# A spectral filter and a low-rank mixer on one core: the start's loads and first-stage work re-ordered

## The chip, the core and the metric

The kernel runs on one core of a Trainium2 chip. A core has a matrix engine (TensorE, PE in the profile), a vector engine (VectorE, DVE), a scalar engine (ScalarE, ACT), a general engine (GpSimd, POOL), a queue processor (SyncE, SP) and 16 DMA engines that all queues share. Each engine runs its own instructions strictly in order; semaphores tie them together. The metric is the device time of one execution in microseconds. Before the change it is 557.71 us, the median of 3 runs (556.44 to 557.84).

## The reference

Two stages on `x` of 8 batches, 3136 positions, 256 channels:

```python
X = np.fft.rfft(x, axis=1)
Y = X * (filt_r + 1j * filt_i)
y = np.fft.irfft(Y, n=3136, axis=1)            # spectral filter
xt = y.transpose(0, 2, 1)
h = xt @ U @ V                                  # low rank over positions, rank 32
u = y + h.transpose(0, 2, 1)
out = u + np.maximum(u @ w_ch1, 0) @ w_ch2      # 256 -> 1024 -> 256
```

Inputs and output are float32; the kernel computes in float16 with float32 sums.

## The kernel before, in words

The length 3136 is split as 64 x 49, and the transform is made in two stages of matmuls.

**First stage** (`f1_units`, L392): 64-point transforms over one factor. The batch's x is loaded in four chunks (`load_x`, L133, two DMAs each, cast to float16 by POOL's queue). 13 units, each one matmul (L401) and one copy out of PSUM (L405 on DVE or L407 on ACT), give the array `c1` in DRAM; when a chunk's units (3, 3, 3 and 4) are done, two DMAs write the chunk (L411), from SP for batch 1 and from POOL for the others.

**Pairs** (`stream`, L462): 16 steps a batch, each for two of 32 residues. `load_a` (L418) brings eight residues in a tile `a2`, on SP's queue. A step makes the 49-point transform (`forward`, L435), the product with the filters on DVE (`both_products`, L443, for batches 0 and 1; `product`, L454 to L459, for the rest) and, two steps later (`LAG`), the inverse 49-point transform `i1` (L471) and its copy (L475). After every fourth pair SP writes the result to `c2` (L477), and `load_e` (L423) reads it back as a quarter of `e2` with two DMAs on SP, when that write has landed.

**Mixer**: `h1_unit` (L497) multiplies all of a batch's e2 with the transformed U (`usb`): 25 matmuls (L502). `make_u` (L544) finishes the inverse transform with the constant `s2` and adds the low-rank part (matmuls L524 and L529, copies L554). `mm1` (L556) and `mm2` (L570) are the two layers of the channel network, in groups of 4 x 128 positions; 6 such groups make a batch, and `out` is written group by group.

**Order.** The schedule is written by hand. First comes batch 0's spectral part by itself: `first_f1`, then `first_mid` (L331), which runs batch 0's 16 pairs without DRAM between: at pair m, the product of m, `back` of m-1 (L345, L348), `ahead` of m+2 and `first_a` of m+3 (L326, L328). The filters come in four parts (`PARTS`); DVE makes their swapped halves before pairs 4, 8 and 12 (L186, L193). Units of batch 1's first stage are put between: `next(fill)`. After pair 15 seven groups of transposes (L382, copies L384) make batch 0's e2, with `prep_u` (L262, transform of U into `usb`) and more units between them. Then batch 0's h1 and first u.

From there the rest runs in slots: two slots go with every two `mm1` tiles, 8 slots a group, `SB` = 48 slots a batch. `put(slot, ...)` hangs a piece of work into a slot: the list `steps` has the slot of each pair; loads of a2 stand some slots ahead of the pair that needs them, `load_e` 3 (batch 1) or 4 slots behind a quarter's last inverse transform, h1 of batch b in slot 48 b - 4, first-stage units of batch b ahead of its pairs, V's arrangement (`vgen`) in slots 1, 3, ..., 11. PE executes the slots in order, so a piece that waits there holds everything behind it. In the text, a(b, g) is the load of a2 for batch b and quarter g, e(b, g) that of e2, "unit" is a unit of the first stage.

The loads of the start stand in one queue on POOL (L196 to L227): batch 0's x, the rest of the filters' rows, then the four parts of filters and tables (`t2`, `g12`), batch 1's x, U, V, w1, w2 and s2. `keep_on(n)` (L280) issues n matmuls of constants whose result is not used.

Of the kernel before, what the change touches and what calls it, by code (L numbers as in the profile page):

```python
# [9 lines left out]
F16 = mybir.dt.float16  # L10
# [7 lines left out]
RANK = 32  # L18
# [68 lines left out]
def kernel(  # L87
# [11 lines left out]
    nc = tc.nc  # L99
# [100 lines left out]
        load_x(0, c)  # L200
    sel = cst.tile([32, 128], F16)
    nc.sync.dma_start(sel, sel_d.ap())
    for k, part in enumerate(PARTS):
        if k == 3:
            for c in range(2):
                load_x(1, c)
        if k:
            load_table(0, *part)
        load_filters(*part)
        if k == 0:  # L210
            load_table(0, *part)
        load_table(1, *part)
    for c in range(2, len(CH)):
        load_x(1, c)
    uq = sb.tile([64, NR * RANK], F16, tag="esb", bufs=2, name="uq")
    nc.gpsimd.dma_start(uq, moe_U.rearrange("(q r) p -> q (r p)", q=NQ))
    vqs = []
    for k in range(2):
        v = sb.tile([32, SEQ // 2], F16, tag="xt", bufs=8, name="vq")
# [1 line left out]
        nc.gpsimd.dma_start(v, moe_V[:, k * (SEQ // 2):(k + 1) * (SEQ // 2)])  # L221
    w1 = cst.tile([128, 2 * 1024], F16)
    nc.gpsimd.dma_start(w1, moe_w_ch1.rearrange("(h dd) c -> dd h c", h=2))
    w2 = cst.tile([128, 8 * DM], F16)
    nc.gpsimd.dma_start(w2, moe_w_ch2.rearrange("(t cc) e -> cc t e", t=8))
    s2 = cst.tile([128, 128], F16)
    nc.gpsimd.dma_start(s2, s2_d.ap())  # L227
    vr = cst.tile([128, NH * 128], F16)
    usb = cst.tile([128, NH * RANK], F16)
    nc.vector.memset(usb[64:128, (NH - 1) * RANK:NH * RANK], 0.0)  # L230
# [31 lines left out]
    def prep_u():  # L262
        for n0, nn in ((0, 16), (16, 9)):
            pu = bank("o", "pu")
            for h in range(2):
                m = (min(nn, NH - h - n0)) * RANK
                a = (h * NH + n0) * RANK
                nc.tensor.matmul(pu[64 * h:64 * h + 64, 0:m], w64[0:64, 0:64], uq[:, a:a + m],
                                 start=True, stop=True)
            m = (min(nn, NH - 1 - n0)) * RANK  # L270
            nc.scalar.copy(usb[:, n0 * RANK:n0 * RANK + m], pu[:, 0:m])
            if m < nn * RANK:
                nc.vector.tensor_copy(usb[0:64, n0 * RANK + m:(n0 + nn) * RANK],
                                      pu[0:64, m:nn * RANK])


# [54 lines left out]
    def first_mid(fill):  # L331

        et = sb.tile([128, 2 * NH * 128], F16, tag="e2", bufs=2, name="et")
        etv = et.rearrange("p (e r h k) -> p h e r k", e=2, h=2, k=64)
        pend = None

        def back(m, uv):
            pi = bank("fx"[m % 2], "pi")
            for sl in range(2):
                for dh in range(2):  # L340
                    for fi in range(2):
                        g = (4 * m + 2 * sl + fi) * 98
                        o = fi * 512 + sl * DM + dh * 128
                        a = (dh * 2 + sl) * 98
                        nc.tensor.matmul(pi[:, a:a + 98], uv[:, o:o + 128], g12[:, g:g + 98],  # L345
                                         start=(fi == 0), stop=(fi == 1), skip_group_check=True)
            for h in range(2):
                nc.scalar.copy(  # L348
                    etv[:, h, :, 0:NH - h, 4 * m:4 * m + 4],
                    pi[:, 0:392].rearrange("p (e k r) -> p e r k", e=2, r=NR)  # L350
                    [:, :, h * NH:h * NH + NH - h])

        def ahead(m):
            return forward(m, st[0]["a"][m // 4], ("m",))

        pxs = [ahead(0), ahead(1)]
        keep_on(8)
        for m in range(NS // 2):
            for k, part in enumerate(PARTS):
                if k and 2 * m == part[0]:  # L360
                    swap_real(*part)
                    swap_imag(*part)
            uv = both_products(m, pxs.pop(0))
            if pend is not None:
                back(*pend)
            pend = (m, uv)
            if m + 2 < NS // 2:
                pxs.append(ahead(m + 2))
            if m + 3 < NS // 2:
                first_a(m + 3)  # L370
            if m >= 7:
                next(fill)
        back(*pend)
        e2 = new_e2(0)
        for k4, n0 in enumerate(range(0, NH, 4)):
            pt = ps.tile([128, 1024], F16, tag="m", bufs=BUFS["m"], name="pe")
            w = min(4, NH - n0)
            k = 64 if w == 1 else 128
            for rr in range(w):
                for dh in range(2):  # L380
                    o, a = rr * DM + dh * 128, (dh * NH + n0 + rr) * 128
                    nc.tensor.transpose(pt[0:k, o:o + 128], et[:, a:a + k], idn[:, :])  # L382
            dst = e2[0:k, n0 * DM:(n0 + w) * DM]
            (nc.scalar.copy if k4 in (1, 4, 6) else nc.vector.tensor_copy)(dst, pt[0:k, 0:w * DM])  # L384
            if k4 == 1:
                prep_u()
            if k4 in (1, 2, 3, 4):
                next(fill)
            if k4 == 5:
                next(vgen)  # L390

    def f1_units(b, both):  # L392
        ne = 0
        for c in range(len(CH)):
            xt = st[b]["x"].pop(c)
            asb = sb.tile([128, 7 * DM], F16, tag="asb", bufs=3, name="asb")
            for n0 in range(0, CH[c], 2):
                w = min(2, CH[c] - n0) * DM
                k = 64 if c0[c] + n0 == NH - 1 else 128
                pf = bank("o" if b == 1 else "m", "pf")  # L400
                nc.tensor.matmul(pf[0:k, 0:w], w64[0:k, 0:k], xt[0:k, n0 * DM:n0 * DM + w],  # L401
                                 start=True, stop=True)
                dst = asb[0:k, n0 * DM:n0 * DM + w]
                if both and ne % 2 and (b > 1 or ne >= 9):
                    nc.vector.tensor_copy(dst, pf[0:k, 0:w])  # L405
                else:
                    nc.scalar.copy(dst, pf[0:k, 0:w])  # L407
                ne += 1
                if n0 + 2 >= CH[c]:
                    for h, o, n in span(c0[c], c0[c + 1]):  # L410
                        (nc.sync if b == 1 else nc.gpsimd).dma_start(c1[b].ap()[:, o:o + n], asb[64 * h:64 * h + 64, 0:n])  # L411
                yield
# [218 lines left out]
    next(h1_unit(0))  # L631
    make_u(0)

    steps = [9 + 1.5 * k for k in range(NP)] + [33 + 2.87 * k for k in range(NP)]
    for b in range(3, nb):
        steps += [SB * (b - 2) + 31 + 3 * k for k in range(NP)]
    steps += [steps[-1] + 3 * (k + 1) for k in range(LAG)]
# [6 lines left out]
    for b in range(1, nb):  # L644
        for gi in range(NS // KG):
            t = steps[NP * (b - 1) + GP * gi]
            put(t - 9, one(load_a, b, gi))
        put(SB * b - 4, h1_unit(b))
        if b > 1:
            fill = f1_units(b, b == 2)  # L650
            for k in range(NF):
                put(4 + 1.1 * k if b == 2 else steps[NP * (b - 1)] - 49 + 3 * k, fill)
            for c in range(len(CH)):
                if b == 2 and c > 1:
                    put(3 * c - 2, one(load_x, b, c))
# [55 lines left out]
```

## Time and profile before

| | |
|---|---|
| median of 3 runs | 557.71 us (556.44 to 557.84) |
| profiled execution | 560.07 us, of which the profile's span is 558.3 us |
| PE busy | 529.5 us (95%) |
| DVE, ACT, POOL busy | 366.9, 363.1, 248.8 us (66%, 65%, 45%) |
| mean granted clock of PE | 0.988 |
| first mm1 matmul (L561) | 56.35 us |
| PE busy from 0 to 55 us | about 37 us |

The slices of the page are 14 us wide, 40 over the span. Lines of a timeline read: start, duration, engine, line, operation, tiles, shapes, and in brackets the engine's idle time before it with what ended the idle time. "SPq" is the issue of a DMA; the transfer itself ends later. Lines of a chain read: start, duration, what.

### The profile page before, as it was taken

Reading aid. Unit: us, or ns where it says so; the run is one execution under the profiler, and the core shown is the slowest. Engines: PE = TensorE matmul, PEld = TensorE weight load, DVE = VectorE, ACT = ScalarE, POOL = GpSimd, SP = SyncE. Lnnn points to the kernel's source line nnn. Section 1 sums busy time; section 2 is a strip of 40 time slices with the busy share of each in tenths; the row PEclk is TensorE's granted clock in tenths of the full one; section 3 lists DMA queues with packets and bytes.
Section 4 is the critical chain, followed back from the end, with each engine's and each line's share of the span. In section 5 each row is a group of like instructions: output and inputs, shape, how many; then the busy total and the mean of one; then the engine's idle time right before and its main releaser. Section 6 shows DMA issues by size and latency. Waiting matters only on the chain.

```text
span 558.3 us, 11590 instructions
## 1 busy us (share of the span) xinstructions
PE 529.5 (95%) x4450; PEld 377.8 (68%) x4450; DVE 366.9 (66%) x531; ACT 363.1 (65%) x731; POOL 248.8 (45%) x357
## 2 busy tenths in 40 slices
PE   4687999999999999999999999999999999999996
PEld 4564467766677767667676766767677767767765
DVE  7875376657777577767777577767777587424342
ACT  3676866767767586767767587677666576654441
POOL 7667440254546455545545465555444334210000
PEclk9969999999999999999999999999999999999998
DMA  8999979769778756786978758786757544541233
GB/s 135 190 188 251 210 160 228 166 155 197 176 184 206 192 135 154 180 201 171 208 177 193 188 138 164 176 208 168 182 150 162 134 116 94 133 90 43 72 77 86
DMA packets 67785, 89.83 MB, mean 161 GB/s; under 512 B 6753, under 2 KB 53378, under 8 KB 66834
## 3 DMA queue, kind: packets, MB, share of 16 engines
q0 software_dynamic: 19152, 50.41, 41.3%
q1 hardware_dynamic: 48498, 38.62, 28.9%
q8 instruction: 35, 0.57, 0.5%
q14 instruction: 20, 0.16, 0.1%
q10 hardware_dynamic: 80, 0.07, 0.0%
HBM read 56.80 MB, written 48.17 MB: 188 GB/s over the span
## 4 chain that ended last, share of the span: by engine, by line
PE 80%; DMA 11%; DVE 4%; ACT 2%; issue 2%; POOL 1%; SPq 0%; ACTq 0%; DVEq 0%; POOLq 0%
PE po L583 29%; PE phh L561 27%; PE pi L471 4%; PE px L435 4%; PE po L587 4%; PE pu L524 4%; PE pu L529 3%; PE pf L401 2%; DMA s<-s2d 2%; DMA xt<-in_x_dram 2%; DMA a<-c 2%; DMA g<-gd 1%; DMA ft<-in_filt_i_dram 1%; DVE uv L456 1%; DVE uv L443 1%
## 5 line engine op out<-in xcount | busy, mean ns | idle before, releaser
L568 ACT ACTIVATE h<-phh 128x512 f16<-128x512 f32 (+1 forms) x350 | 186.2, 575 | 105.4 <-PE phh L561 105.4
L583 PE MATMUL po<-w,h 128*128 128x256 f16 x1568 | 203.2, 273 | 0.0
L561 PE MATMUL phh<-ut,w 128*128 128x512 f16 x768 | 197.5, 379 | 0.3 <-ACT ut L554 0.2
L459 POOL TENSOR_TENSOR y<-uv 128x512 f16<-128x512 f16 x96 | 110.2, 1148 | 150.4 <-DVE uv L456 72.8
L583 PEld LDWEIGHTS <-h 128*128 128x128 f16 x1568 | 150.0, 98 | 35.8
L456 DVE TENSOR_TENSOR uv<-px,ft 64x512 f16<-64x512 f32 x192 | 132.0, 688 | 2.6
L592 DVE COPY och<-po 128x512 f32<-128x512 f32 x96 | 66.4, 692 | 79.7 <-PE po L587 78.2
L561 PEld LDWEIGHTS <-w 128*128 128x128 f16 x832 | 74.4, 97 | 52.7 <-issue 3.1
L454 DVE TENSOR_TENSOR uv<-px,ft 128x512 f16<-128x512 f32 x96 | 66.0, 687 | 55.1 <-PE px L435 53.1
L475 ACT CAST esb<-pi 98x512 f16<-98x512 f32 x112 | 65.7, 587 | 40.0 <-PE pi L471 31.9
L600 POOL DMA_DIRECT2D out_dram<-och x84 | 45.4, 546 | 64.0 <-DVE och L592 64.0
L407 ACT CAST asb<-pf 128x512 f16<-128x512 f32 (+1 forms) x83 | 47.6, 573 | 17.8 <-PE pf L401 17.8
L566 DVE TENSOR_SCALAR h<-phh 128x512 f16<-128x512 f32 (+1 forms) x66 | 42.9, 649 | 20.1 <-PE phh L561 19.6
L554 ACT CAST ut<-pu 128x512 f16<-128x512 f32 x96 | 51.8, 598 | 2.9 <-PE pu L529 2.6
L435 PE MATMUL px<-a,t 98*128 98x256 f16 x256 | 49.9, 277 | 4.1 <-ACT a L328 0.9
L587 PE MATMUL po<-idn,ut 128*128 128x128 f16 x384 | 52.8, 219 | 0.0
L443 DVE TENSOR_TENSOR uv<-px,ft 128x1024 f16<-128x1024 f32 x32 | 38.2, 1219 | 12.7 <-PE px L435 12.4
L529 PEld LDWEIGHTS <-e 128*128 128x128 f16 (+1 forms) x400 | 30.9, 97 | 18.6 <-issue 3.4
L524 PE MATMUL pu<-vr,h 128*128 128x512 f16 (+1 forms) x112 | 39.6, 354 | 1.4 <-ACT h L506 0.5
L529 PE MATMUL pu<-s,e 128*128 128x128 f16 (+1 forms) x400 | 40.3, 218 | 0.5 <-DMA s<-s2d 0.5
L587 PEld LDWEIGHTS <-ut 128*128 128x128 f16 x384 | 37.5, 98 | 4.4
L136 POOL DMA_DIRECT2D xt<-in_x_dram x64 | 34.4, 542 | 8.9 <-DMA xt<-in_x_dram 3.0
(73 smaller groups left out, 364.2 us busy)
## 6 DMA issues: line engine op xcount, KB each, us to landing
out_dram<-och POOLq DMA_DIRECT2D x84, 256.0 KB, 4.2
a<-c SPq DMA_DIRECT2D x28, 392.0 KB
c<-esb SPq DMA_DIRECT2D x28, 392.0 KB
xt<-in_x_dram POOLq DMA_DIRECT2D x56, 192.0 KB, 5.9
c<-asb POOLq DMA_DIRECT2D x42, 192.0 KB, 3.2
e<-c SPq DMA_DIRECT2D x28, 200.0 KB
e<-c SPq DMA_DIRECT2D x28, 192.0 KB
out_dram<-och SPq DMA_DIRECT2D x12, 256.0 KB
```

What stands on the lines that cost most here:

```text
L435: nc.tensor.matmul(px[:, sl * DM:(sl + 1) * DM], t2[:, s * 128:(s + 1) * 128], a2[:, (2 * ml + sl) * DM:(2 * ml + sl + 1) * DM], start=Tru ...
L454: nc.vector.tensor_mul(uv[:, 0:512], px[:, :], ft[:, a:a + 512])
L456: nc.vector.tensor_mul(uv[p:p + 64, 512:1024], px[q:q + 64, :], ft[q:q + 64, b:b + 512])
L459: nc.gpsimd.tensor_add(y, uv[:, 0:512], uv[:, 512:1024])
L475: nc.scalar.copy(esb[:, ml * 512:(ml + 1) * 512], pi[0:98, :])
L524: nc.tensor.matmul(pm[:, o:o + nr * k], h1[:, dh * 128:(dh + 1) * 128], vr[:, r0 * 128:r0 * 128 + nr * k], start=True, stop=False, skip_gr ...
L529: nc.tensor.matmul(pm[:, o + rr * k:o + (rr + 1) * k], e2[0:k, a:a + 128], s2[0:k, 0:k], start=False, stop=(rr == nr - 1), skip_group_chec ...
L561: nc.tensor.matmul(pm[:, 0:w], w1[:, dh * 1024 + t * 128:dh * 1024 + (t + 1) * 128], ut[:, dh * w:(dh + 1) * w], start=(dh == 0), stop=(dh ...
L568: nc.scalar.activation(h[:, 0:w], pm[:, 0:w], RELU)
L583: nc.tensor.matmul(po[:, o:o + DM], hs[gx, t][:, rr * 128:(rr + 1) * 128], w2[:, t * DM:(t + 1) * DM], start=(t == 0), stop=False, skip_gr ...
L587: nc.tensor.matmul(po[:, o + dh * 128:o + (dh + 1) * 128], ut[:, dh * w + rr * 128:dh * w + (rr + 1) * 128], idn[:, :], start=False, stop= ...
L592: nc.vector.tensor_copy(och[:, a:(rr + 1) * DM], po[:, 0:(rr + 1) * DM - a])
```

## The change

Six things are changed together.

1. The order of the start's loads on POOL: of batch 1's x one chunk, not two, stands ahead of the last part of the filters; chunk 1 comes behind U, chunk 2 behind w1, chunk 3 behind w2. `s2` is loaded by SP near the beginning.
2. In `first_mid`, 12 keep-on matmuls at pairs 3, 7 and 11; `prep_u` at pair 14 instead of among the transposes, its last copy on ACT instead of DVE.
3. Units of batch 1's first stage: six (pairs 9, 10, 11, 14, 15, and one among the transposes) instead of thirteen in the start; the other seven in slots 0 to 6, with PSUM tiles of the kind "m".
4. Batch 1's pairs from slot 14 by 1.4 (before: 9 by 1.5), batch 2's from 36.5 by 2.7 (before: 33 by 2.87).
5. The loads of a2 stand 6 (batch 1) or 8 slots ahead of their pair, before 9.
6. Batch 2's first-stage units stand in slots 8 to 20, before in 4 to 17.

```diff
+    s2 = cst.tile([128, 128], F16)
+    nc.sync.dma_start(s2, s2_d.ap())
     for k, part in enumerate(PARTS):
         if k == 3:
-            for c in range(2):
-                load_x(1, c)
+            load_x(1, 0)
...
-    for c in range(2, len(CH)):
-        load_x(1, c)
     uq = sb.tile([64, NR * RANK], F16, tag="esb", bufs=2, name="uq")
     nc.gpsimd.dma_start(uq, moe_U.rearrange("(q r) p -> q (r p)", q=NQ))
+    load_x(1, 1)
...
     nc.gpsimd.dma_start(w1, moe_w_ch1.rearrange("(h dd) c -> dd h c", h=2))
+    load_x(1, 2)
     w2 = cst.tile([128, 8 * DM], F16)
     nc.gpsimd.dma_start(w2, moe_w_ch2.rearrange("(t cc) e -> cc t e", t=8))
-    s2 = cst.tile([128, 128], F16)
-    nc.gpsimd.dma_start(s2, s2_d.ap())
+    load_x(1, 3)
...
             if m < nn * RANK:
-                nc.vector.tensor_copy(usb[0:64, n0 * RANK + m:(n0 + nn) * RANK],
+                nc.scalar.copy(usb[0:64, n0 * RANK + m:(n0 + nn) * RANK],
...
-            if m >= 7:
+            if m in (3, 7, 11):
+                keep_on(12)
+            if m in (9, 10, 11, 14, 15):
                 next(fill)
+            if m == 14:
+                prep_u()
...
-            if k4 == 1:
-                prep_u()
-            if k4 in (1, 2, 3, 4):
+            if k4 == 3:
                 next(fill)
...
-                pf = bank("o" if b == 1 else "m", "pf")
+                pf = bank("o" if b == 1 and ne < 6 else "m", "pf")
...
-                if both and ne % 2 and (b > 1 or ne >= 9):
+                if both and ne % 2 and (b > 1 or ne > 6):
...
-    steps = [9 + 1.5 * k for k in range(NP)] + [33 + 2.87 * k for k in range(NP)]
+    steps = [14 + 1.4 * k for k in range(NP)] + [36.5 + 2.7 * k for k in range(NP)]
+    for k in range(7):
+        put(k, fill)
...
-            put(t - 9, one(load_a, b, gi))
+            put(t - (6 if b == 1 else 8), one(load_a, b, gi))
...
-                put(4 + 1.1 * k if b == 2 else steps[NP * (b - 1)] - 49 + 3 * k, fill)
+                put(8 + k if b == 2 else steps[NP * (b - 1)] - 49 + 3 * k, fill)
```

## The prediction

> **What bounds the kernel now.** I read the page first (busy shares, slices), then the chain that ended last, then the timeline of its first 60 us, then the SP queue's timeline, and last the landings and packets of the DMAs. TensorE (PE) carries the span:
>
> ```profile
> PE 529.5 (95%) x4450; PEld 377.8 (68%) x4450; DVE 366.9 (66%) x531; ACT 363.1 (65%) x731; POOL 248.8 (45%) x357
> PE   4687999999999999999999999999999999999996
>
> ```
>
> PE is full from slice 5 on; only the first four slices (to 56 us) and the last are not. So a microsecond counts in three ways: the moment the first L561 matmul starts (56.35 us), the PE work put behind that moment, and any wait of PE behind it. The chain of the start:
>
> ```profile
> 33.77 7.95 DMA g<-gd
> ...
> 43.63 11.62 DMA s<-s2d
> 55.29 0.40 PE pu L529 x4
> 55.71 1.08 ACT ut L554 x2
> 56.84 0.81 PE phh L561 x3
> ```
>
> The start is a queue of loads: each DMA of POOL lands behind the one before. The landings give the price of each item: a chunk of batch 1's x 1.45 to 1.85 us, t2 1.35, a part's four filters 3.1, g 2.0, U 1.2, V 1.5, w1 3.5, w2 2.9. The timeline shows what waits for them:
>
> ```profile
> 39.86 0.71 DVE L193 TENSOR_SCALAR ft<-ft 64x2048 f16<-64x2048 f16 x1 [0.93 <-DMA ft<-in_filt_i_dram]
> 40.68 4.62 DVE L443 TENSOR_TENSOR uv<-px,ft 128x1024 f16<-128x1024 f32 x4
> ...
> 46.65 1.07 PE L382 MATMUL pe<-idn,et 128*128 128x128 f16 x16 [0.77 <-ACT et L348]
> ...
> 48.71 0.87 ACT L271 CAST usb<-pu 128x512 f16<-128x512 f32 x2
> 49.35 0.38 PE L401 MATMUL pf<-xt,w 128*128 128x512 f16 x1 [1.19 <-ACT usb L271]
> ```
>
> The last filters open pairs 12 to 15; then come the transposes to e2, U's transform and four units of the first stage (L401) between them. Behind the start, I looked for the waits nearest to what the change moves. Batch 1's spectrum goes out by SP (L477), comes back as e2 (L427), and h1 of batch 1 (L502) needs all of it:
>
> ```profile
> 99.86 0.33 SPq L477 DMA_DIRECT2D c<-esb  x1
> 103.05 0.77 SPq L427 DMA_DIRECT2D e<-c  x2
> ...
> 109.56 0.33 SPq L477 DMA_DIRECT2D c<-esb  x1
> 114.03 0.79 SPq L427 DMA_DIRECT2D e<-c  x2
> ```
>
> ```profile
> 119.97 0.92 PE L502 MATMUL ph<-e,usb 128*32 128x256 f16 x25 [0.67 <-ACT esb L475]
> ...
> 246.88 0.92 PE L502 MATMUL ph<-e,usb 128*32 128x256 f16 x25 [0.18 <-DMA e<-c]
> ```
>
> The read at 114.03 starts when the write of 109.56 has landed; its last packet ends at 118.96. PE takes it up at 119.97, so h1(1) has 1 us to spare, and h1(3) at 246.88 already waited for its read. That spare is what the change spends.
>
> **The change, part by part.** All sums are against the profiled execution, 560.07 us (span 558.3 and 1.8 around it). It is 2.4 above the median of the runs, 557.71, so a difference of the sum is added to the median.
>
> *Loads of x, s2.* One chunk of x instead of two stands ahead of the last part: filters land 1.85 us earlier (39.77 to 37.9), g too (41.73 to 39.9). Products 12 to 15 then run from about 38.8 to 43.4 instead of 40.7 to 45.3. Past w1 only one chunk has been passed beside U and V, so w1 lands near 48 (52.2 before), far ahead of need. s2 by SP lands in the first microseconds; the 0.54 us that PE waited for it at 55.29 goes. Chunk 1 of x now lands behind g and U: 39.9 + 1.2 + 1.45, and 0.5 for the write of c1's first chunk beside it, near 43.1. Chunks 2 and 3 land near 49.7 and 55, their units stand in slots 0 and 3 (55 and 57): no wait, 0.5 at worst. POOL reaches V's copies some 3 us earlier (they began with V's landing, 47.98), so vr's units, at slot 1 and on as before, have more spare.
>
> *Keep-alive matmuls at pairs 3, 7, 11.* 36 matmuls in places where PE waits anyhow (2.06 us idle before 26.88). They should keep the clock, which was at half from 26.35 to 36.59. Pairs 8 to 11 lie before the filter wait, so this earns nothing on the path; if the cover goes, 12 matmuls cost 0.85 us a place (8 took 0.61).
>
> *Units 3 and 4 at pairs 14 and 15, U at pair 14.* PE reaches unit 3 at about 41.6 and waits for chunk 1 to 43.1, with U and the last two inverse transforms queued behind it. Then ScalarE (ACT) does one unit copy, U's two (0.87) and its tail (0.2, taken from DVE), pair 14's, a unit's, pair 15's: at 0.48 from start to start (43.67, 44.15, 44.58 in the timeline) 3.1 us, so transposes begin near 46.7, as before. The 1.9 us won from the filters are used up here.
>
> *Transposes without U and with one unit.* The stretch from 46.65 to e2's last copy (53.57) took 6.9 us. Out go the 1.2 us of waiting for U's copies and two unit copies on ACT, 0.84: 4.9 remains. With s2's 0.54, the start moves from 56.35 to about 53.8 to 54.2: gain 2.3 us. Bounds: 0.5 if chunk 1 lands at 44.9, 4.5 if it lands before it is needed.
>
> *Seven units into slots 0 to 6.* Batch 2's units move from slots 4-17 to 8-20 in return. Slots 0 to 7 are ACT's (it is busy 5.00 of 5.00 us from 60 to 65): three full copies and a short one come, two go: 0.75 us. Four more of batch 2's matmuls fall behind slot 8, where PE is full: 4 x 0.21 = 0.85. Sum 1.6, bounds 1.4 (PE's work of seven units alone) to 2.4. Their DMAs move too: SP writes c1's chunks 1 to 3 after unit 5, slot 2 and slot 6 instead of all before the start, with batch 1's loads of a2 behind them on SP (below); POOL writes batch 2's c1 three to four slots later, still nine slots ahead of a(2,0).
>
> *Pairs from slot 14, then 36.5.* With two pairs of lag, batch 1's last inverse transform moves from slot 36 (33 + 2.87) to slot 39 (36.5 + 2.7). h1(1) stays in slot 44. Before, its transform started at 108.47 and the spectrum's write 1.1 us later. From there the chain to e2's last packet takes: over the 28 such chains of this trace 6.9 to 11.5 us; for batch 1 10.95, 10.5, 7.5 and 9.4, the higher two with a load of a2 issued beside the write. The change puts load a(2,1) into slot 39 too, right behind the write, so I take 10.1. PE's own work from that write to h1 is slots 40 to 44 (113.33 to 118.73) less 0.45: 4.95 us. So PE, with all later work behind it in its queue, waits 10.1 + 0.1 - 4.95 = 5.2 us; bounds 2.0 (6.9) and 6.7 (11.5). In exchange slot 44 holds no pair any more, and the 0.67 us of 119.97 goes.
>
> *The clock behind that wait.* The clock's records here turn at multiples of 3.41 us (26.35 to 36.59 is three), and one turned to half after a window with PE busy 1.57 of 3.41 and a gap of 2.06. A 5.2 us wait makes such a window wherever it falls. PE then runs at half until a full window has passed: 1.5 to 4.9 us of work at half, loss 0.75 to 2.45; I take 1.7. Nothing if the wait is near 2.
>
> The Trainium skill, "TensorE: Matmul & The Clock Gate", section "What's actually happening", says that the clock halves after at least one idle window of about 3.4 us. The trace has the window's length but halved it without a fully idle one. By that rule a 5.2 us wait would cost clock in half of the alignments only, and the sum without the loss would be 561.5.
>
> *Loads of a2 at 8 or 6 slots.* a(1,0) is issued when c1's last chunk has landed: 8 us from the start for slot 6 and its copy, 3.2 to 5.5 for the write, 3.0 for the load, 14.2 to 16.5, against pair 0 at 17.4: nothing, 1 at worst. From batch 3 on the load follows SP's write in the same moment as before: nothing, or some 0.3 where spare is least (1.3 us for a(4,1)). a(2,2) loses one slot of a distance after which PE already waited 0.49 (at 137.06): up to 1.0, taken as 0, as other such loads took 2 to 4 us less.
>
> *DVE.* Unit 7 goes to it; pairs and batch 2's odd units overlap in slots 14-20 instead of 9-17; the two waits of PE for it (0.38, 0.39) stay or go.
>
> Sum: -2.3 + 1.6 + 5.2 - 0.67 + 1.7 = +5.5 us. Profiled execution 565.6, median 563.2.
>
> **Rivals.**
> *No wait at slot 44.* If write and read come through in 4.95 us, -2.3 + 1.6 - 0.67 - 0.4 (half of DVE's waits): 555.9, faster. It decides from a chain of 4.95 us down; against it stands that the shortest of 28 is 6.9, on an idle queue at the end; for it, that PE's pause frees the DMA engines.
> *Clock kept.* The wait as priced but the clock full: 561.5.
> *More is late.* Chain at 11.5 us, two windows at half, a(1,0) and a(2,2) late: 5.2 + 1.5 for the wait, 1.7 more for the clock, 1 to 2 for the loads: 567 to 569. For it: several rows already at 1 us of spare.
> *The start gives its most.* Gain 4.5, wait 2.0, no clock loss: -4.5 + 1.6 + 2.0 - 0.67 = -1.6: 556.1, within 0.3%. Against it: unit 3 in PE's queue ahead of U.
>
> **How the numbers follow.** Forecast as summed 0.45, clock kept 0.20, more is late 0.20, no wait 0.10, the start's most 0.05. A difference under 0.3% (1.7 us) can hardly be told from none. No wait gives faster 0.08 and same 0.02, the start's most same 0.05; the other three are all slower: 0.85. The range leaves out the last two cases below (0.15) and the dearest quarter of "more is late" above (0.05): 558.5 to 568.5.
>
> **What would show it.** First L561 near 54 us; half clock gone from 26 to 36; the fill at pair 14 waiting for x; L502 for batch 1 with about 5 us of wait put down to the read of e2, and a record of half clock behind it; slots 0 to 7 a little longer. I am wrong if L502 waits under 2 us, or the start moves by more than 5.

## The result and the profile after

The change makes the kernel slower, and by more than the range held: 573.09 us, the median of 6 runs (571.06 to 577.91), against 557.84 for 6 runs of the kernel before beside them (556.44 to 560.27). The ratio is 1.0281 with a 95% interval of 1.0237 to 1.0326. The forecast was 563.2 (558.5 to 568.5).

The profiled execution took 572.36 us, its span 570.6. First the page: busy times and the first two rows of slices that answer to those shown of before. Slices are 14.3 us wide.

```profile
PE 536.9 (94%) x4486; PEld 383.3 (67%) x4486; DVE 367.8 (64%) x531; ACT 362.8 (64%) x731; POOL 247.6 (43%) x356
...
PE   5778999939999999999999999999999999999996
...
PEclk9997999987999999999999999999999999999998
```

The start is fuller (5778 for 4687), as forecast. New is the 3 in the ninth slice, 114 to 128 us, and the 8 and 7 of the granted clock around it. The timeline of PE names it (start, duration, line, tiles, and in brackets the idle time before):

```profile
52.36 0.39 PE L526 MATMUL pu<-vr,h 128*128 128x512 f16 x1 [0.48 <-ACT h L508]
...
53.65 1.30 PE L563 MATMUL phh<-ut,w 128*128 128x512 f16 x4 [0.23 <-ACT ut L556]
...
56.16 0.39 PE L252 MATMUL pv<-vp,sel 32*128 32x512 f16 x1 [0.79 <-DVE asb L407]
...
127.59 1.65 PE L504 MATMUL ph<-e,usb 128*32 128x256 f16 x25 [9.01 <-DMA e<-c]
```

L563 is the mm1 matmul that was L561, and L504 is h1, that was L502: all lines behind the first edit stand two lower. The first mm1 matmul starts at 53.65 (before 56.35). h1(1) waits 9.01 us for the read of e2; before, it waited 0.67, for another thing. The chain of work around it shows what the 9 us consist of:

```profile
113.81 5.68 DMA c<-esb
119.48 0.02 issue
119.50 0.32 SPq L429
119.86 7.45 DMA e<-c
127.32 0.28 issue
127.59 1.65 PE ph L504 x23
```

The write to `c2` takes 5.7 us, the read behind it 7.45. The windows around the wait (stretch and length, then the busy time of PE, PEld, DVE, ACT and POOL with counts, the granted clock, the share and rate of the DMA engines):

```profile
118.60:127.60 9.00, 0.01 (x2) 0.04 (x2) 1.16 (x2) 0.60 (x1) 1.07 (x1) 0.79 0.74 153
127.60:134.10 6.50, 6.50 (x53) 4.57 (x54) 0.00 (x0) 1.82 (x4) 0.00 (x0) 0.50 0.00 0
134.10:145.00 10.90, 10.90 (x86) 7.65 (x85) 8.51 (x13) 8.04 (x16) 5.54 (x7) 1.00 0.51 139
```

In the first stretch PE stands still and the other engines are busy for 0.6 to 1.2 us; what runs is the transfer. In the second, PE works without a gap at half clock, 6.5 us long.

A ledger of the two profiled executions, by when the first mm1 matmul of a slot starts, after minus before:

| place | after minus before, us | what changed there |
|---|---|---|
| first mm1 (slot 0) | -2.70 | the start |
| slot 44 | -0.12 | +2.58: seven units, pairs, waits for copies |
| slot 46 | +10.96 | +8.34 of waiting (9.01 less 0.67), +2.74 of half clock |
| slot 96 | +12.51 | +1.55: among it one pair more behind slot 46 (0.44), a wait of 0.58 for a(3,1) |
| end | +12.30 | |

The start varies between executions, as will be seen; the time from the first mm1 matmul to the end hardly does. It was 501.9 us in the first profiled execution of before and 501.4 in a second, 516.9, 517.7 and 516.6 in three of after. The change therefore costs 14.7 to 16.3 us behind the start, where the forecast had 7.8 (5.5 and the start's 2.3).

### The profile page after: what moved, and what is told of

The parts are those of the page before. It is cut to its first block, busy times and chain, and to the rows that moved or that the text cites. A ratio compares the mean times of both kernels' runs of the same rounds, so it can differ in the third digit from the quotient of the medians.

```text
span 570.6 us, 11653 instructions
## 1 busy us (share of the span) xinstructions
PE 536.9 (94%) x4486; PEld 383.3 (67%) x4486; DVE 367.8 (64%) x531; ACT 362.8 (64%) x731; POOL 247.6 (43%) x356
## 4 chain that ended last, share of the span: by engine, by line
PE 79%; DMA 5%; DVE 4%; ACT 2%; issue 1%; POOL 0%; SPq 0%; ACTq 0%; DVEq 0%
PE po L585 29%; PE phh L563 27%; PE px L437 4%; PE pi L473 4%; PE pu L526 4%; PE po L589 4%; PE pu L531 4%; PE pf L403 3%; DMA a<-c 2%; DVE uv L458 2%; DMA e<-c 1%; PE ph L504 1%; DMA c<-esb 1%; DVE uv L456 1%; ACT h L570 1%
## 5 line engine op out<-in xcount | busy, mean ns | idle before, releaser
L563 PE MATMUL phh<-ut,w 128*128 128x512 f16 x768 | 197.5, 379 | 0.4 <-ACT ut L556 0.2
L563 PEld LDWEIGHTS <-w 128*128 128x128 f16 x832 | 74.7, 97 | 52.9 <-issue 3.2
L409 ACT CAST asb<-pf 128x512 f16<-128x512 f32 (+1 forms) x82 | 46.7, 570 | 14.4 <-PE pf L403 14.4
L413 POOL DMA_DIRECT2D c<-asb x48 | 25.9, 546 | 35.5 <-ACT asb L409 32.5
```

The costliest lines, as they stand in the source:

```text
L563: nc.tensor.matmul(pm[:, 0:w], w1[:, dh * 1024 + t * 128:dh * 1024 + (t + 1) * 128], ut[:, dh * w:(dh + 1) * w], start=(dh == 0), stop=(dh ...
```

## Experiments

**One line alone.** The largest term of the forecast sum was the wait at h1(1). If it comes from where batch 1's pairs end, that line put into the kernel before must bring it without any other part of the change.

```diff
-    steps = [9 + 1.5 * k for k in range(NP)] + [33 + 2.87 * k for k in range(NP)]
+    steps = [9 + 1.5 * k for k in range(NP)] + [36.5 + 2.7 * k for k in range(NP)]
```

> The kernel before with one thing of the change: batch 2's pairs from slot 36.5 by 2.7, so that batch 1's last inverse transform stands in slot 39 and h1 of batch 1 still in slot 44. Theory A (the distance from that transform to h1 is too short for the write and read of e2): L502 for batch 1 waits 5 to 9 us, half clock behind it, time 565 to 570. Rival B (the wait comes from the rest of the change: the order of the loads, the seven units in slots 0 to 6, batch 2's units in slots 8 to 20): the wait stays under 2.5 us and the time within 3 us of before, 557 to 561.

Measured: 568.63 us (567.73 to 569.88), ratio 1.0182 (1.0149 to 1.0214). SP's queue, and PE at h1(1) with the clock around it:

```profile
113.20 0.33 SPq L477 DMA_DIRECT2D c<-esb  x1
...
118.52 0.87 SPq L427 DMA_DIRECT2D e<-c  x2
```

```profile
125.77 1.65 PE L502 MATMUL ph<-e,usb 128*32 128x256 f16 x25 [7.79 <-DMA e<-c]
```

```profile
118.00:125.80 7.80, 0.03 (x4) 0.06 (x8) 1.15 (x2) 0.60 (x1) 1.06 (x1) 0.63 0.94 155
125.80:130.30 4.50, 4.50 (x43) 2.97 (x43) 0.00 (x0) 1.59 (x4) 0.00 (x0) 0.51 0.07 12
```

The line brings a wait of 7.79 us and 4.5 us at half clock. Its execution lost 8.9 us between slots 44 and 46 of the 9.2 by which its end is later; slot 44 itself came 0.40 us sooner after the first mm1 matmul than in before (60.93 for 61.33), as fewer pairs stand ahead of it. The late pairs are enough for most of the slowdown: theory A holds, B falls.

**The whole change with the old end of the pairs.** Here everything stays but the pairs, which run from slot 14 by 1.25 and later end where they did before.

```diff
-    steps = [14 + 1.4 * k for k in range(NP)] + [36.5 + 2.7 * k for k in range(NP)]
+    steps = [14 + 1.25 * k for k in range(NP)] + [33.4 + 2.86 * k for k in range(NP)]
```

> The changed kernel with its pairs closer together, from slot 14 by 1.25 and from 33.4 by 2.86, so that batch 1's last inverse transform stands in slot 36 as before; the load of a(2,1) is still right behind the write on SP. Theory A: wait of L502 for batch 1 under 2 us, no half clock behind it, 557 to 560 (the start gained 2.7 us in the profile, the units cost some 2.6 by slot 40). Rival C (the wait comes from a(2,1) standing between write and read on SP, wherever they are): still 3 us of wait or more and 562 or more.

Measured: 565.75 us (564.16 to 570.87), ratio 1.0158 (1.0095 to 1.0221). The mechanism is gone, the time is not:

```profile
121.20 0.93 PE L504 MATMUL ph<-e,usb 128*32 128x256 f16 x25 [1.13 <-DMA e<-c]
```

h1(1) waits 1.13 us, at full clock, and the clock's record shows no half between 48 and 560 us. But from the first mm1 matmul to slot 44 this execution needs 4.13 us more than before (after: 2.58). Up to slot 10 it is as long as after; the difference comes behind it, where the pairs are denser: PE waits for DVE's products four times, 0.17 to 0.88 us, 1.8 in all (after: twice, 0.8), and one more of batch 2's pairs (0.44) stands ahead of slot 44. The load a(2,2) is then waited for 1.94 us, a(3,0) 0.54. The time expected was missed: what the change puts ahead of slot 44 cost more than the forecast's 1.6 in both places of the pairs.

**What stretches the write and the read.** The forecast took 10.1 us from the issue of the write to e2's last packet; the chain was 13.8. In the profile two loads stand near it. SP issues a(2,1) right behind the write, and POOL issues the last chunk of batch 3's x, x(3,3), in slot 41:

```profile
113.81 0.33 SPq L479 DMA_DIRECT2D c<-esb  x1
114.18 0.52 SPq L422 DMA_DIRECT2D a<-c  x1
119.50 0.78 SPq L429 DMA_DIRECT2D e<-c  x2
```

```profile
116.34 1.08 POOL L136 DMA_DIRECT2D xt<-in_x_dram  x2
```

x(3,3)'s packets run from 118.84 to 126.36 and the read's from 121.95 to 126.81; a(2,1)'s last packet comes at 122.45. Four kernels, all with the whole change otherwise, separate the two loads and the clock. First a(2,1) issued behind the read instead of ahead of it:

```diff
-            put(t - (6 if b == 1 else 8), one(load_a, b, gi))
+            put(43 if (b, gi) == (2, 1) else t - (6 if b == 1 else 8), one(load_a, b, gi))
```

> The changed kernel with the load a(2,1) moved from slot 39 to slot 43, behind the read e(1,3) on SP's queue; the transform stays in slot 39. Theory A: the chain gets the time of the rows without a load beside it (7.5 to 9.5 us instead of 13.0), so the wait of 9.0 us falls to 3 to 5, with half clock still behind it: 567 to 570. Rival C: with nothing between write and read the wait falls under 2 us: 562 or less.

Then x(3,3) in slot 46 instead of 41, alone and together with the edit above:

```diff
-                    put(steps[NP * (b - 1)] - 68 + 10 * c, one(load_x, b, c))
+                    put(46 if (b, c) == (3, 3) else steps[NP * (b - 1)] - 68 + 10 * c, one(load_x, b, c))
```

> The changed kernel with one load moved: x(3,3), the last chunk of batch 3's x on POOL's queue, from slot 41 to slot 46, so that it is issued behind the read e(1,3) and not 3 us ahead of it. Theory E (the read is slow because x(3,3) stands on the DMA engines ahead of it; in the changed kernel the read's first row starts 2.45 us after its issue, before 0.95): the read takes 4 to 5.5 us instead of 7.3, the wait of L502 for batch 1 falls from 9.0 to 6 to 7.5 us, time down by 1.5 to 3. Rival F (the queue's own a(2,1) is what holds it): the read stays at 7 us and the wait at 8.5 to 9.5.

> The changed kernel with both moved behind the read e(1,3): x(3,3) to slot 46 and a(2,1) to slot 43. The chain of write and read is then bare but for the output and c1. Theory E with a share for a(2,1): chain 8.5 to 10 us, wait 3.5 to 5.5 us, which is what the prediction had; time 565 to 568. Rival F: the same as with a(2,1) alone moved (wait 8.5), 569 or more.

Measured, with the pieces of each chain in the profiled executions (from the issue of the write; "first row" is from the read's issue to the start of its first packet):

Each ratio is to executions of before taken beside that kernel (median 557.84 us for after, 560.11 for the two kernels with x(3,3) moved, 558.86 for the others), so the medians of two rows cannot simply be subtracted.

| kernel | median us | ratio (95%) | write | first row | read | write to h1 | wait of h1(1) |
|---|---|---|---|---|---|---|---|
| before | 557.84 | 1 | 4.47 | 0.96 | 4.93 | 10.41 | 0.67 (by ACT) |
| after | 573.09 | 1.0281 (1.0237 to 1.0326) | 5.70 | 2.45 | 7.31 | 13.79 | 9.01 |
| late pairs alone | 568.63 | 1.0182 (1.0149 to 1.0214) | 5.32 | 2.07 | 6.21 | 12.57 | 7.79 |
| a(2,1) behind | 569.66 | 1.0203 (1.0158 to 1.0248) | 4.75 | 2.51 | 7.08 | 13.24 | 8.46 |
| x(3,3) later | 569.73 | 1.0173 (1.0136 to 1.021) | 5.62 | 1.05 | 5.62 | 12.22 | 7.44 |
| both | 567.24 | 1.0117 (1.0074 to 1.016) | 4.74 | 0.93 | 3.70 | 10.07 | 5.29 |

The queue of the kernel with both edits, and its h1(1):

```profile
116.42 0.33 SPq L479 DMA_DIRECT2D c<-esb  x1
121.17 0.87 SPq L429 DMA_DIRECT2D e<-c  x2
122.13 0.36 SPq L422 DMA_DIRECT2D a<-c  x1
126.49 1.65 PE L504 MATMUL ph<-e,usb 128*32 128x256 f16 x25 [5.29 <-DMA e<-c]
```

The last two columns settle the size of the wait. Whatever stood in the way, PE's work between the write's issue and h1(1) was 4.78 us in all five with the late pairs (13.79 - 9.01, 12.57 - 7.79, 10.07 - 5.29), near the forecast's 4.95. With both loads out of the way the chain is 10.07 and the wait 5.29. That these are close to the forecast's 10.2 and 5.2 is luck: the forecast had a(2,1) in its chain, and 0.1 us from the last packet to PE where 1.63 passed here (4.74 + 3.70 + 1.63). a(2,1) lengthens the write by about 0.9 us; x(3,3) lengthens the time to the read's first packet by 1.4 to 1.6. The read itself falls from 7.3 to 3.7 only when both are gone; with one of them moved it takes 5.6 or 7.1.

Two expectations were missed. With a(2,1) moved the wait was 8.46 us instead of 3 to 5 (the profile names a2's load for its end, which is issued right behind the read; h1 reads no a2). With x(3,3) moved the read took 5.62 us where 5.5 was the most. And the two loads do not explain every long write: in late pairs alone no load of a2 is issued between the write and the read and the write took 5.32 us, and in the mended kernel (below) neither load is, and it took 6.31 and 5.68. What stretches those was not tested.

**The clock behind the wait.** h1(1) waits as before, but PE multiplies constants meanwhile; their results are not used.

```diff
     def h1_unit(b):
...
+        if b == 1:
+            keep_on(140)
```

> The changed kernel with 140 matmuls of constants (7.8 us at full clock) just ahead of L502 of batch 1, that is inside the wait. The wait for e2 itself stays where it ends (about 127.6 us in the profile). If the half clock from 123.85 to 134.09 costs what it looks like (6.5 us of work at half, 3.2 us), that record is gone and the time falls by 2.5 to 3.5, to about 570. If the clock costs nothing on the path (the work behind is held by something else), the time stays at 573.

Measured: 568.01 us (566.97 to 569.82), ratio 1.0172 (1.0138 to 1.0207). PE around h1(1), and the windows:

```profile
118.39 7.99 PE L285 MATMUL keep<-idn,w 128*128 128x128 f16 x140
...
128.25 0.93 PE L506 MATMUL ph<-e,usb 128*32 128x256 f16 x25 [1.87 <-DMA e<-c]
```

```profile
118.50:128.30 9.80, 7.93 (x144) 7.79 (x147) 1.16 (x2) 0.60 (x1) 1.07 (x1) 1.00 0.75 143
128.30:134.10 5.80, 5.80 (x68) 4.30 (x68) 2.06 (x3) 3.66 (x8) 0.00 (x0) 1.00 0.01 3
```

The clock stays full, and h1's 25 matmuls take 0.93 us instead of 1.65. The delay is not shorter (7.99 + 1.87 = 9.86 us, as its chain was 14.55), so what is saved is the clock alone. The ratio fell from 1.0281 to 1.0172, some 6 us, more than the 2.5 to 3.5 expected; in the profiled executions the time from the first mm1 matmul to the end fell by 2.5 (516.9 to 514.5), which is the clock's share. Slot 44 to 46 took 16.86 us in after and 14.72 here; less their delays, 7.85 and 4.86, so half the clock cost 2.99. Against before, 5.78 less 0.67, it is 2.74. What it costs depends on where the wait falls against the clock's records: by the same working the second and third executions of after (below) lost 1.5 and 1.4.

**Which copies hold the first slots.** Of the seven late units' copies, the change gives DVE three (units 7, 9 and 11) and ACT four; this kernel gives DVE all seven.

```diff
-                if both and ne % 2 and (b > 1 or ne > 6):
+                if both and (ne % 2 if b > 1 else ne >= 6):
```

> The changed kernel with the copies of all seven moved units on DVE (of them three are there, four on ACT). Theory G (slots 0 to 7 are bound by ACT, which is why the start's 2.7 us shrink to 1.3 by slot 8): slot 8 comes 7.2 to 8.2 us behind the first L563 matmul instead of 8.9, and 0.7 to 1.5 us of time are won. Rival H (PE's own matmuls for the units cost it): slot 8 stays within 0.3 us of 8.9.

Measured: 570.75 us (566.76 to 574.82), ratio 1.0191 (1.0119 to 1.0263). From the first mm1 matmul to slot 8 its profiled execution took 9.01 us, after's 8.88, before's 7.50. ACT's copies alone are not what bounds these slots: theory G falls. The number is the one that H named, but H's cause is not shown. PE was busy for 7.87 of the 9.01 us, in after for 7.96 of 8.88, in before for 7.25 of 7.50; so of the 1.4 us that the change costs here about half is PE's work and the rest waits, and with all copies on DVE PE waited for DVE instead, 0.57, 0.21 and 0.25 us.

**The start's clock.** After has a record of half clock from 41.93 to 48.76, over the transposes (32 of them in 3.43 us). This kernel fills PE's gaps at pairs 12 and 13.

```diff
-            if m in (3, 7, 11):
+            if m in (3, 7, 11, 12):
                 keep_on(12)
+            if m == 13:
+                keep_on(6)
```

> The changed kernel with 12 more matmuls of constants at pair 12 and 6 at pair 13. In the changed kernel the clock turns to half from 41.93 to 48.76 us, with the transposes in it (32 in 3.43 us). If that half clock is on the path of the start, the record is gone, the transposes take about 2.2 us and the first L563 matmul comes at 52.2 to 53.0 instead of 53.65; if ACT's copies hold the start anyway, it comes at 53.4 to 53.9. The median moves by no more than 1.5 us either way.

Measured: 572.75 us (569.91 to 574.38), ratio 1.0221 (1.0176 to 1.0266). The edit did only half of what it was for: the record of half is 3.41 us long here instead of 6.83 (43.93 to 47.34), and nearly all of the 32 transposes still lie in it (3.30 us from 43.57 on). The first mm1 matmul starts at 51.71, which by itself says little: eleven executions of the start of after lie between 50.07 and 56.27. But measured from the first transpose (L386) these eleven sort themselves by the clock. First after, then its second execution (below), which has no half clock there:

```profile
45.64 3.43 PE L386 MATMUL pe<-idn,et 128*128 128x128 f16 x32 [0.64 <-ACT et L348]
...
53.65 1.30 PE L563 MATMUL phh<-ut,w 128*128 128x512 f16 x4 [0.23 <-ACT ut L556]
```

```profile
44.35 1.96 PE L386 MATMUL pe<-idn,et 128*128 128x128 f16 x32 [1.01 <-ACT et L348]
...
50.89 1.30 PE L563 MATMUL phh<-ut,w 128*128 128x512 f16 x4 [0.23 <-ACT ut L556]
```

The three without half clock over the transposes (this one, x(3,3) later, all copies on DVE) take 6.54, 6.55 and 6.54 us from the first transpose to the first mm1 matmul; the eight with it take 7.17 to 9.06. So that half clock does lie on the start's path and costs 0.6 to 2.5 us. The rest of the spread lies ahead of the transposes: the last filters are in place (L193) between 36.21 and 39.66 us. The execution with PE's gaps filled also waited 2.76 us for a later batch's e2, at 320.2, with 3.41 us of half clock behind it.

**The change mended.** Pairs as in the second experiment, x(3,3) later, and the loads of a2 10 and 9 slots ahead for batches 2 and on.

> The changed kernel with three things mended: pairs from slot 14 by 1.25 and from 33.4 by 2.86 (last inverse transform of batch 1 in slot 36), x(3,3) in slot 46, the loads of a2 10 slots ahead for batch 2 and 9 from batch 3 on. If the loss lay in the late chain, its clock and the a2 loads alone, what is left is the earlier start (-2.7 in the profile) against the moved units and denser pairs (back36 stood 1.4 behind before at slot 44): L502 of batch 1 waits under 0.5 us, the pair that waited 1.94 us for a(2,2) in back36 waits under 0.7, and the time is that of before within 0.7%, 557 to 562. If the earlier start is worth what the sum of the prediction gave it, it is 1 us better than before; if it comes out above 563, there is a loss that none of the runs has shown.

Measured: 565.59 us (562.79 to 571.54), ratio 1.0104 (1.0065 to 1.0142), above what was expected. h1(1) waits 2.69 us in the profiled execution, which was the longest of its runs, and 2.54 in a second one. That second one, 568.55 us, shows where else time goes:

> The mended kernel once more. From its first L563 matmul to slot 44 65.5 us (61.3 in the kernel before: moved units and denser pairs, 4.1 us); if that is all of its loss, its span is that of before plus 4.1 less what its start is earlier, and waits for e2 stay under 1 us; if waits that come and go carry it, one of more than 1 us shows.

```profile
252.97 1.65 PE L504 MATMUL ph<-e,usb 128*32 128x256 f16 x25 [3.41 <-DMA e<-c]
```

```profile
238.02 0.33 SPq L479 DMA_DIRECT2D c<-esb  x1
238.45 0.47 SPq L422 DMA_DIRECT2D a<-c  x1
246.52 0.78 SPq L429 DMA_DIRECT2D e<-c  x2
```

h1(3), which waited 0.18 us in before, waits 3.41 here: 8.5 us passed from the write's issue to the read's. With the half clock behind it (251.65 to 258.48) the delay against before grows from 2.9 us (slot 140) to 8.5 (slot 142). The first execution had none of it there but 3.39 at 382.3, again with half clock. These waits come and go between executions, and I have not found what sets them off.

**Parts that might gain.** s2 by SP, put alone into the kernel before:

```diff
+    s2 = cst.tile([128, 128], F16)
+    nc.sync.dma_start(s2, s2_d.ap())
     for k, part in enumerate(PARTS):
...
-    s2 = cst.tile([128, 128], F16)
-    nc.gpsimd.dma_start(s2, s2_d.ap())
```

> The kernel before with one part of the change: s2 loaded by SP in the first microseconds instead of as the last item of POOL's queue. The wait of 0.54 us of the first u (L529) for s2 is gone, and nothing else moves: 0.3 to 0.7 us faster, which is below what the measurement tells from none (0.3%). If the start is held by something beside it (h1, V's copies), no wait is gone and the first L561 matmul stays at 56.0 to 56.5.

12 runs, 557.95 us (556.48 to 560.23), ratio 0.9978 (0.9954 to 1.0001). The 0.54 us of waiting for s2 is gone, but the time can hardly be told from none. The keep-on matmuls alone:

```diff
+            if m in (3, 7, 11):
+                keep_on(12)
             if m >= 7:
                 next(fill)
```

> The kernel before with one part of the change: 12 matmuls of constants at pairs 3, 7 and 11. The prediction said that they keep the clock (half from 26.35 to 36.59 in the profile of before) and earn nothing on the path, because pairs 12 to 15 wait for the last filters: no half clock between 25 and 37 us, first L561 matmul within 0.7 us of 56.35, time within 0.3%. Rival: the clock is on the path (PE made pairs 10 and 11 late by 1.27 and 0.49 us): first L561 matmul 1 to 2 us earlier.

12 runs, 560.18 us (557.69 to 567.51), ratio 1.0043 (1.001 to 1.0076). Its profile has no half clock between 25 and 37 us. That does not show that these matmuls hold the clock, for three other executions with the start of before and without them have none there either (the second one of before below, late pairs alone, s2 by SP). The median is 0.4% higher, just outside the 0.3% expected, for no reason that was found. The first mm1 matmul came at 54.27, earlier than expected, but the second execution of before has it at 54.05; from the last filters (L193) to it 16.41 us pass, in the two executions of before 16.49 and 16.63. So the matmuls earn nothing on the path. All that looked useful together, in the kernel before (s2 by SP, keep-on, x(3,3) in slot 46, batch 2's loads of a2 11 slots ahead):

> The kernel before with what the runs speak for: s2 by SP, the keep-on matmuls at pairs 3, 7 and 11, x(3,3) in slot 46 and batch 2's loads of a2 11 slots ahead of their pairs; units, U and pairs stay as before. If the parts add up: 0.5 to 1.7 us for the start, 0.7 for h1 of batch 1, 0.5 for a(2,2): 1.5 to 3 us faster than before, ratio 0.995 to 0.998. If they are all hidden: 0.998 to 1.002.

12 runs, 559.69 us (557.96 to 565.55), ratio 1.0022 (0.999 to 1.0053): no gain; its h1(1) waited 1.75 us, with 3.41 us of half clock behind it (118.97 to 122.39). Nothing tried beats the kernel before beyond doubt.

**Again, both kernels.** One more execution of before and two of after tell what of the 15 us belongs to single executions.

> The kernel before once more, one profiled execution. If the first one (560.07 us, 2.2 above the median) was long because of its start, the first L561 matmul now comes at 54 to 55.5 us instead of 56.35 and the rest keeps its length to within 0.7 us. If the start is fixed, it comes at 56.0 to 56.6 and the difference lies behind it.

> The changed kernel once more. Start between 51.7 and 56.3 us (the spread of the other runs with its code); from the first L563 matmul to slot 44 63.9 us as before, to 0.3; wait of L502 for batch 1 8.5 to 9.5 us and half clock behind it. If the rest of the loss lies in later waits for e2 or a2 that come and go, one shows with more than 1 us.

> The changed kernel a third time; the same as for the second.

| execution | time us | first mm1 | first mm1 to end | wait of h1(1) | write to h1 |
|---|---|---|---|---|---|
| before, first | 560.07 | 56.35 | 501.9 | 0.67 | 10.41 |
| before, second | 557.25 | 54.05 | 501.4 | 0.99 | 10.72 |
| after, first | 572.36 | 53.65 | 516.9 | 9.01 | 13.79 |
| after, second | 570.4 | 50.89 | 517.7 | 8.89 | 13.68 |
| after, third | 572.5 | 54.17 | 516.6 | 8.80 | 13.58 |

The wait is there each time and of one size. The start of after's second execution came below the range expected (50.89 for 51.7). Later waits of over 1 us showed, one in each repeat: 1.17 for e2 at h1(3) in the second, 1.38 for a load of a2 at 257.39 in the third. The first profiled execution of before was 2.2 us above the median of its runs, and 2.3 us of it lay in its start (56.35 against 54.05).

## Why the prediction was right and wrong

The direction, the place and the mechanism were right: h1(1) waits for e2's read, the waiting gate is the write and read behind batch 1's last quarter, and half clock follows. The size was not. Against the sum of +5.5 us on the profiled execution stand 12.3 us:

| term | forecast (bounds) | measured |
|---|---|---|
| start | -2.3 (-4.5 to -0.5) | -2.70 |
| seven units in slots 0 to 6 | +1.6 (1.4 to 2.4) | +2.58 by slot 44 |
| wait at h1(1), less 0.67 | +4.5 (1.3 to 6.0) | +8.34 |
| half clock | +1.7 (0.75 to 2.45) | +2.74 (later executions 1.5 and 1.4) |
| loads of a2, DVE and the rest | 0 (to 1.0) | +1.34 |

**The step that failed** is the chain in "Pairs from slot 14, then 36.5": "so I take 10.1", with 0.1 from there to PE. It measured 13.79 all told (13.01 to e2's last packet, 0.78 behind it), 3.6 us more. PE's work beside it was 4.78 for 4.95, so the wait came out 3.8 longer. The figure came from 28 chains of the trace before, of which the longest was 11.5; I took that for a bound. I counted a(2,1), which the change moves to the write, and not x(3,3), which the change doesn't move: the chain moved to it. Taking x(3,3) away shortened the chain by 1.57 us, a(2,1) by 0.55, both by 3.72; and with a(2,1) alone left beside it the chain still took 12.22, 2.0 more than the 10.2 in which it was counted.

The old trace could have told this, if write and read had been priced apart. In five of its 28 chains a load of a2 is issued right behind the write and a load of x between the write and the read. One of them (the second row is a2's load, the last the load of x):

```profile
205.17 0.33 SPq L477 DMA_DIRECT2D c<-esb  x1
205.56 0.51 SPq L420 DMA_DIRECT2D a<-c  x1
208.75 0.78 SPq L427 DMA_DIRECT2D e<-c  x2
```

```profile
207.59 1.07 POOL L136 DMA_DIRECT2D xt<-in_x_dram  x2
```

In these five the read's first packet came 2.2 to 2.9 us after its issue and the read took 5.9 to 7.2 us, much as here. Their sums were only 9.8 to 10.9, because four of the writes took 3.3 to 3.6 us and the fifth 5.06. Other writes of that trace took up to 6.66. The longest write and the longest read together, 13.9, would have bounded the 13.01; the longest sum, 11.5, did not. Why the write was short in four of the five and long here, the runs do not show.

The reading that "h1(1) has 1 us to spare" was wrong too, and the 0.1 us from the last packet to PE with it. In all profiled executions 0.78 to 1.63 us lie between e2's last packet and h1(1), also where PE waits for nothing but the read; so the 1.01 of before were hardly spare. In the second execution of before h1(1) waits for the read itself:

```profile
117.98 0.92 PE L502 MATMUL ph<-e,usb 128*32 128x256 f16 x25 [0.99 <-DMA e<-c]
```

**The clock** was mis-sized for this execution, not in its mechanism. Half lasted from 123.85 to 134.09, three times 3.41 us. By these records a window ended at 130.67 in which PE was busy from 127.59 on, 3.08 of 3.41 us; the clock came back only after the next. So 6.5 us of work ran at half, where the forecast's most was 4.9. Other alignments gave 4.0 and 3.7 us (second and third execution of after) and 4.5 (late pairs alone), inside its bounds, and there the loss was 1.4 to 1.5 us, near the 1.7 taken. The Trainium skill, "TensorE: Matmul & The Clock Gate", section "What's actually happening", puts the throttle behind an idle window of about 3.4 us, and by that rule the rival "clock kept" had its 0.20. A wait of 9 us holds one idle window however it falls, so for after the trace agrees with the rule. For shorter waits it does not. With both loads moved h1(1) waits from 121.20 to 126.49, about as long as forecast, and the clock is at half from 123.51 to 130.33, though neither window of 3.41 us that the wait touches (120.10 to 123.51, 123.51 to 126.92) is idle throughout; and waits of 1.75 us (all that looked useful together) and 2.54 us (the mended kernel) were followed by half clock too. So the rival fell with the length of the wait, and the runs speak against it at the forecast's length as well.

**The seven units**, with the pairs, cost 2.58 by slot 44, a little above the upper bound, although the late pairs alone reach that slot 0.40 sooner than before; without that it is nearer 3.0. Part is the 0.79 us at 56.16, in which V's matmul stands behind a unit's copy on DVE; by slot 10 the forecast's 0.75 was 1.34. With the denser pairs of the second experiment it was 4.13.

**The start** came out as forecast, 53.65 for 53.8 to 54.2, and the wait for s2 is gone, but luck has a part in it. PE waited for x at the fill only 0.35 us, to 41.68, not to 43.1, so the transposes began at 45.64 instead of 46.7; and half clock over them, which the forecast did not have, took about 1.5 us of that back (8.01 us to the first mm1 matmul, 6.54 without it). That the keep-on matmuls take the half clock away is not shown: its place differs from one execution to the next also without them, 26.35 to 36.59 in the first execution of before and 39.67 to 43.08 in the second.

**The base.** The sum was made on one profiled execution and its difference "added to the median". That execution of before had a late start: 2.3 of the 2.9 us by which its span exceeds the second one's lie ahead of the first mm1 matmul. Between the profiled executions the change costs 12.3 us, between the medians 15.25: the rest is 2.2, by which before's profile lies above its median, and 0.7, by which after's lies below. Three executions of the old start (both of before, late pairs alone) have the first mm1 matmul at 55.5 us on average and eleven of the new one at 53.1, but as either spreads by more than 2 us, the new start's worth can't be told more closely than 1 to 3.

**The rivals.** "More is late" came nearest, at 567 to 569; it had the longer wait, the clock over two windows and late loads of a2, yet a chain of 11.5 us only. "No wait at slot 44" and "the start gives its most" fell with the 9.01 us. Neither of the two signs that were to show it wrong came; a wait that is too long was not among them.

**What stays open.** The mended kernel is 5.8 us above before, and its wait at h1(1), 2.5 to 2.7 us, is less than half of that. It needs 4.1 us more than before ahead of slot 44, against which stands the start's gain; the rest varies with waits for e2 of later batches, whose cause was not found. Nor is it known why the write took 5.2 to 6.3 us in kernels with no load of a2 issued right behind it, nor how much of a window PE must work for full clock.

## What to carry to other kernels

Price a transfer that you move by what it will stand beside at its new time, on every queue: a load that is not touched by the change can be the one that it now meets. Price the pieces of a chain apart, here the write and the read: the longest sum in the old trace is no bound when the longest pieces never met there. When PE is already behind a DMA, every microsecond by which the chain grows comes back in full (write to h1 less the wait was 4.78 us in all five kernels of the table with the late pairs), and a wait that drops the clock is paid again in part. And measure behind a noisy start from a fixed event, not from zero: the starts of this case spread over 6 us from zero, and the three with full clock agree to 0.01 us from their first transpose.

## What was not expected of the hardware

- A read issued on SP while a load of POOL's queue was in flight started later: with x(3,3) ahead of it the first packet came 2.07 to 2.53 us after the issue, with x(3,3) moved 0.93 to 1.42. The Trainium skill, "DMA: Bandwidth & Descriptors", section "Issuing engines are not separate DMA queues", says that transfers of all queues run on the same 16 engines and interleave; the trace agrees, as x(3,3)'s packets (118.84 to 126.36) and the read's (121.95 to 126.81) run beside each other in after, and a read that takes 3.70 us with both loads out of the way takes 7.31.
- 3.08 us of work in a window of 3.41 (127.26 to 130.67 in after) did not bring the full clock back, while 2.77 did in the start of the kernel with a(2,1) behind (45.14 to 48.55). So one and the same wait costs 1.4 or 2.7 us of clock from one execution to the next, and the busy time of PE alone does not say which.
- Waits of PE as short as 1.75 us were followed by a record of half clock 3.41 us long, one of 1.94 us (at 140.19 in the second experiment) by none.
- The same start took from 50.07 to 56.27 us to the first mm1 matmul in eleven profiled executions, while what follows repeats within 1.1 us for the same kernel (516.6 to 517.7).
- Between e2's last packet and the matmul that waits for it lay 0.8 to 1.6 us.
